# A planner's price table set anew: transposes, 1 MB loads, long ScalarE passes, strided copies, short products

## The chip, the cores and the metric

One core of a Trainium2 chip. The core has TensorE (PE in the profile, its weight loads PEld), VectorE (DVE), ScalarE (ACT), GpSimd (POOL) and SyncE (SP), which issues the DMAs. The metric is the device time of one launch in microseconds (us), as the median of several runs. The kernel computes in f32 accuracy with f16 products: a value is scaled by a power of two and held as a high and a low f16 half.

## The reference

Causal attention over 4 batches, 8 heads, 576 positions and 64 columns a head, with a bias, then two layers of a feed-forward kind on the 2304 resulting rows:

```
scores = q @ k.T / sqrt(64) + min(-(cum[i] - cum[j]), 0)       # cum = cumsum(max(s, 0)); causal
x = softmax(scores) @ v                                        # rows: 4 * 576 = 2304, columns: 8 * 64 = 512
h = x @ w_in ;  x2 = (h - tanh(h)) @ w_out                     # w_in 512 x 2048, w_out 2048 x 512
out = ((x2 @ w_a) * (x2 @ w_b)) @ w_out2                       # w_a, w_b 512 x 1536, w_out2 1536 x 512
```

The inputs are f32 or 64-bit arrays in DRAM; the weights arrive as 64-bit numbers, which the kernel turns into f32 itself.

## The kernel before

The work is a list of some thousands of operations, written out by `tile_attention_two_moes`: attention units (a batch and a pair of heads, in two parts: query blocks 0 and 1, and the later "merged" units with query blocks 2, 3 and the tail of 64), nine blocks of 256 rows through the first layer (`l1_mm`, `l1_act`, `l2_mm`), and five blocks of up to 512 rows through the second (`l3_mm`, `l3_act`, `l4_mm`, and `seven`, which computes products of a 2 x 2 split with seven instead of eight sub-products). Each weight is loaded in slots of 1 MB (`fetch`: the load, a pass that shifts the low halves, which may run on ScalarE or VectorE, a long pass on ScalarE, a joining pass on VectorE), squared on ScalarE for its scale, and split in two halves (`w_split`). `w2_done` closes the preparation of the second layer's weights; the products of the second layer wait for it. The second layer's weights live in a pool (`late`) that opens when the pool of the merged attention units (`rest`) has been used up.

In a unit, `u_split` makes the halves of q and k in the tile `qk`, a DMA transpose turns it into `qkT` (`u_turn`), a copy `kB` takes part of it, `u_qk` forms scores in PSUM, `u_exp` the exponentials (one block goes to the SBUF tile `zs`, the tail's lie in `z`), `u_norm` writes the two f16 halves to `a` (or `am` for the tail) by `copy_scaled` and `lo_part`, a second DMA transpose makes `aT` (`aTm`), and `u_pv` multiplies with `v` into 64 partitions of PSUM. `copy_scaled`, `lo_part` and `small` record calls that may run on one of two or three engines (`pl.either`).

No order is written out by hand. `Plan.record` stores each operation with what it depends on, a due time and its price from `cost` (line 575): how long it holds its engine, how long after that its result can be used (the lag), and for DMAs the time of the bytes. `Plan.run` (line 382) simulates the engines: of the operations that are ready on an engine, the one with the earliest due time that has its buffers goes next; for a call with several engines, `best` compares the time at which each would be through with it, by price times a weight (`WV`, `WV2` 1.2 for VectorE, `WP` 1.1 for GpSimd, 1 for ScalarE). For a DMA the lines are

```python
dma = max(dma, now + op.dur + 650.0) + op.size
end = dma
```

and what reads the result may start at `end + op.lag`. The order of this simulation is the order in which the instructions are issued on the chip, where each engine works through its own in that order and waits by semaphores.

Before the last simulation `Plan.refine` (line 322) goes through the list `REFINE`. For each step (gap, mix, shake, seed) it simulates the plan forwards, then backwards (`backward`, which finds the latest start of each operation, with `gap` added to the lags), and `move` shifts the due times by `mix` of the way to those latest starts and by a random amount of size `shake`; steps with a seed of 300 or more do so in a random stretch of time.

Of the kernel before, what the change touches and what calls it, by code (L numbers as in the profile page):

```python
# [12 lines left out]
F16 = mybir.dt.float16  # L13
# [21 lines left out]
MASKED = -1.0e34  # L35
BLOCKS = [(p, [b]) for p in range(2) for b in range(4)]
TURN = 0.0
REFINE = [(1000.0, 0.2, 0.0, 195), (1000.0, 0.1, 1000.0, 258), (200.0, 0.1, 1000.0, 286), (0.0, 0.1, 0.0, 402), (-200.0, 0.2, 1000.0, 73372), (100.0, 0.0, 2000.0, 21910), (100.0, 0.1, 3000.0, 984), (400.0, 0.5, 2000.0, 64535), (200.0, 0.1, 300.0, 792), (0.0, 0.0, 300.0, 70647), (2000.0, 1.0, 3000.0, 55229), (200.0, 0.0, 1000.0, 70112), (0.0, 0.05, 3000.0, 681), (-200.0, 0.0, 1000.0, 932), (2000.0, 0.1, 0.0, 724), (2000.0, 1.0, 0.0, 19448), (200.0, 0.0, 3000.0, 7485), (2000.0, 0.0, 2000.0, 26392), (400.0, 0.0, 1000.0, 851), (-200.0, 0.2, 300.0, 65873), (100.0, 0.0, 2000.0, 94663), (2000.0, 0.1, 300.0, 616), (400.0, 0.1, 0.0, 673), (2000.0, 0.2, 1000.0, 52138), (200.0, 0.5, 3000.0, 38807), (400.0, 0.0, 300.0, 20859), (100.0, 0.2, 0.0, 48173), (200.0, 0.3, 1000.0, 702), (200.0, 0.0, 300.0, 86139), (200.0, 0.05, 300.0, 39857)]
SEVEN = 12
GSB = (1,)  # L40
ZSB = 0
# [486 lines left out]
class _Eng:  # L528
# [3 lines left out]
    def __getattr__(self, what):  # L532
        plan, name = self.plan, self.name

        def call(*args, reads=(), writes=(), **kw):
            rd, wr = [], []
            for i, a in enumerate(args):
                if isinstance(a, View):
                    (wr if i == 0 else rd).append(a)
            for k, a in kw.items():  # L540
                if isinstance(a, View):
                    (wr if k in ("out", "accum_out") else rd).append(a)
            def real(a):
                assert not isinstance(a, View) or a.buf.real is not None, (name, what, a.buf.name, a.buf.tag)
                return a.real() if isinstance(a, View) else a

            def fn():
                return getattr(getattr(plan.nc, name), what)(  # L548
                    *[real(a) for a in args], **{k: real(a) for k, a in kw.items()})

            fn.what = (name, what)
            fn.lock = shares(name, what, rd, wr)
            dur, lag, size = map(round, cost(name, what, rd, wr, kw, args))
            plan.record(name, fn, rd, wr, reads, writes, dur, lag, size, plan.shift.get(name, 0.0))

        return call
# [18 lines left out]
def cost(eng, what, rd, wr, kw, args):  # L575


    def count(v):
        n = 1
        for d in v.shape[1:]:  # L580
            n *= d
        return n

    if not rd and not wr:
        return 500.0, 900.0, 1000.0
    main = wr[0] if wr else rd[0]
    n = max(count(v) for v in rd[:1] + wr[:1])
    if eng == "sync":
        rows = main.p1 - main.p0
        size = {F32: 4, I32: 4}.get(main.dtype, 2)  # L590
        b = rows * count(main) * size
        if what == "dma_start_transpose":
            return 650.0, 910.0, b / 292.5
        hold = 475.0 if rows in (32, 128) else 625.0
        return hold, 910.0, b / (180.0 if main.shape[-1] * size < 512 else 360.0)
    if eng == "tensor":
        lhs = rd[0]
        rate = 4.0 if lhs.dtype == F32 else 1.0
        cols = count(main)
        half = 0.62 if main.p1 - main.p0 == 64 else 1.0  # L600
        return max(cols * rate / 2.4 * half, 25.0) + 2, 200.0, 0
    psum = any(v.buf.pool == "ps" for v in rd)
    small = sum(isinstance(kw.get(k), View) for k in ("scale", "bias", "scalar", "scalar1", "scalar2"))
    if what == "tensor_scalar_mul" and isinstance(args[2], View):
        small += 1
    if eng == "vector":
        if what == "reciprocal":
            return 65 + 8 * n, 127.0, 0
        if what == "tensor_tensor_scan":
            return 65 + n, 127.0, 0  # L610
        fast = what.startswith("tensor_scalar") or what in ("tensor_single_scalar", "tensor_copy", "memset")
        rate = 0.96
        if fast and not psum:
            rate = 3.84 if rd and rd[0].dtype == F16 else 1.92
        return 69 + n / rate + 60 * small + 8 * ("accum_out" in kw), 127.0, 0
    if eng == "scalar":
        d = (52 if psum and not small else 94) + n / 1.2 + 93 * ("accum_out" in kw)
        return d + small * (51 if psum else 93), 153.0, 0
    if what == "tensor_tensor":
        return 149 + 1.9 * n, 80.0, 0  # L620
    if what == "tensor_scalar":
        return 190 + 83 * small + 0.833 * n, 80.0, 0
    if what == "memset":
        return 210.0, 80.0, 0
    return 70 + 1.45 * n, 80.0, 0
# [3 lines left out]
def tile_attention_two_moes(  # L629
# [1051 lines left out]
    with tc.manual_schedule():  # L1681
        pl.refine(REFINE)
        pl.run(switch)
# [34 lines left out]
```

## Time and profile before

| what | value |
|---|---|
| median of 3 runs | 1008.97 us (1007.15 to 1009.83) |
| the profiled execution's own time | 1005.35 us |
| its span, first to last instruction | 1003.5 us |
| TensorE busy | 916.8 us (91%) |
| VectorE busy | 815.2 us (81%) |
| ScalarE busy | 551.0 us (55%) |
| GpSimd busy | 148.6 us (15%) |
| granted TensorE clock, mean | 0.991 |
| DMA | 113.95 MB, mean 114 GB/s |

The span in 40 equal slices of 25 us; each digit is a busy share in tenths:

```
PE   1697889998989878989999989999999999999998
DVE  8698999979899989899999999999267559546545
ACT  6699668658768678778598764433022212222221
POOL 2033031102123212321001010020011002000000
```

TensorE is nearly full from 600 us on, where VectorE has room after 700 us; from 50 to 600 us both are close to full.

### The profile page before, as it was taken

To read this page: it belongs to the slowest core of one execution; us is meant where nothing else is said; L and a number is where in the kernel's file an instruction comes from. 1 tells how busy PE (TensorE), PEld (TensorE's weight loads), DVE (VectorE), ACT (ScalarE), POOL (GpSimd) and SP (SyncE) were. 2 spreads that over 40 slices of the span, in tenths; PEclk is the share of its full clock that TensorE was granted. 3 is DMA by queue.
4 is the path that set the end of the run, shared out by engine and by line. 5 is a ranking of instruction groups with operands and counts; after the bars stand their busy time and mean duration, and the time that the engine had idled before them with its cause. 6 is when DMAs were issued, how large, how long until landed. Compare 5 with 4: busy or idle time off the path is not lost.

```text
span 1003.5 us, 20812 instructions
## 1 busy us (share of the span) xinstructions
PE 916.8 (91%) x7998; PEld 689.4 (69%) x7998; DVE 815.2 (81%) x2058; ACT 551.0 (55%) x1097; POOL 148.6 (15%) x239
## 2 busy tenths in 40 slices
PE   1697889998989878999989999999999999999998
PEld 0485678887767756778778887644467777777675
DVE  8698999979899989999899999999267559546545
ACT  6699668658768678777598764433022212222221
POOL 2033031102123212321001010020011002000000
PEclk9997899999999999999999999999999999999999
DMA  8999767557986997996755530200011011000001
GB/s 227 221 329 225 184 109 140 104 113 152 177 161 129 194 183 158 181 181 135 233 171 198 180 106 2 63 22 1 1 42 43 1 43 42 1 2 12 32 1 43
DMA packets 282084, 113.95 MB, mean 114 GB/s; under 512 B 251200, under 2 KB 265776, under 8 KB 281984
## 3 DMA queue, kind: packets, MB, share of 16 engines
q1 hardware_dynamic: 281984, 112.62, 48.6%
q8 instruction: 62, 1.02, 0.4%
q14 instruction: 38, 0.31, 0.1%
HBM read 60.53 MB, written 11.17 MB: 71 GB/s over the span
## 4 chain that ended last, share of the span: by engine, by line
PE 39%; DVE 11%; ACT 4%; DMA 4%; issue 3%; SPq 0%; POOL 0%; DVEq 0%; POOLq 0%; ACTq 0%
PE h L548 14%; PE qk L548 12%; PE acc L548 8%; PE pv L548 6%; DVE w L548 2%; DVE xf L548 2%; ACT w L548 2%; DVE ghl L548 1%; DVE a L548 1%; DMA w<-in_moe_w_a_dram 1%; DVE qk L548 1%; DVE h L548 1%; DMA w<-in_moe_w_out_dram 1%; ACT xf L548 1%; DVE am L548 1%
## 5 line engine op out<-in xcount | busy, mean ns | idle before, releaser
L548 PEld LDWEIGHTS <-w 128*128 128x128 f16 x5160 | 498.5, 98 | 133.3 <-issue 30.2
L548 PE MATMUL h<-xhl,w 128*128 128x256 f16 (+1 forms) x2256 | 289.7, 279 | 3.9 <-DVE xhl L548 1.7
L548 PE MATMUL acc<-ghl,w 128*128 128x256 f16 x1536 | 187.6, 272 | 5.5 <-DVE ghl L548 2.2
L548 PE MATMUL h<-xf,w 128*128 128x256 f16 (+1 forms) x560 | 87.8, 306 | 0.7 <-ACT bits L548 0.4
L548 PEld LDWEIGHTS <-ghl 128*128 128x128 f16 x432 | 42.3, 98 | 44.6
L548 PEld LDWEIGHTS <-qkT 128*128 128x128 f16 (+2 forms) x352 | 28.5, 102 | 58.6 <-issue 33.5
L548 DVE CUSTOM_DVE_ANT_0 qk<-qk,caus,cs 128x384 f32<-128x384 f32 (+2 forms) x120 | 64.6, 555 | 2.2 <-PE qk L548 1.9
L548 PE MATMUL qk<-qkT 128*128 128x128 f16 (+4 forms) x168 | 45.7, 316 | 21.2 <-DMA qkT<-qk 7.6
L548 ACT ACTIVATE sq<-h 128x512 f32<-128x512 f32 x36 | 21.5, 597 | 78.2 <-PE h L548 78.2
L548 PE MATMUL acc<-w,ghl 128*128 128x512 f16 x252 | 60.9, 379 | 0.0
L548 ACT ACTIVATE qk<-qk,nm 128x512 f32<-128x512 f32 (+3 forms) x88 | 45.8, 521 | 18.7 <-DVE nm L548 15.1
L548 ACT ACTIVATE w<-w 128x1024 f32<-128x1024 f32 (+1 forms) x43 | 49.2, 1161 | 8.0 <-DMA w<-in_moe_w_out_dram 3.1
L548 ACT ACTIVATE th<-h,xc 128x512 f32<-128x512 f32 x64 | 43.9, 686 | 15.3 <-PE h L548 9.8
L548 DVE SCALAR_TENSOR_TENSOR a<-qk,sm,a 128x512 f16<-128x512 f32 (+3 forms) x88 | 48.8, 574 | 3.2 <-ACT a L548 2.9
L548 PE MATMUL qk<-kB,qkT 67*128 67x128 f16 (+4 forms) x168 | 45.5, 313 | 4.2 <-ACT kB L548 2.0
L548 ACT ACTIVATE sq<-raw 128x576 bf16<-128x576 f32 (+2 forms) x57 | 38.6, 679 | 18.1 <-DMA raw<-in_v_dram 7.5
L548 PEld LDWEIGHTS <-v 128*64 128x64 f16 x1440 | 38.4, 113 | 14.6 <-issue 13.2
L548 DVE TENSOR_TENSOR g<-g,h 128x512 f32<-128x512 f32 x36 | 24.4, 684 | 23.7 <-PE h L548 23.4
L548 PE MATMUL qk<-w,ghl 128*128 128x512 f16 x180 | 43.6, 379 | 0.0
L548 PE MATMUL pv<-aT,v 128*64 128x128 f16 x960 | 36.0, 225 | 5.3 <-DMA aT<-a 4.2
L548 ACT ACTIVATE bits<-h,cpc 128x512 f32<-128x512 f32 x18 | 12.4, 687 | 50.6 <-DVE g L548 37.7
L548 PEld LDWEIGHTS <-sq 128*128 128x128 f16 (+1 forms) x234 | 22.8, 98 | 23.9 <-ACT sq L548 0.8
(260 smaller groups left out, 1691.4 us busy)
## 6 DMA issues: line engine op xcount, KB each, us to landing
w<-in_moe_w_out_dram SPq DMA_DIRECT2D x8, 1024.0 KB
w<-in_moe_w_in_dram SPq DMA_DIRECT2D x6, 1024.0 KB
x_d<-x2hl SPq DMA_DIRECT2D x18, 256.0 KB
raw<-in_k_dram SPq DMA_DIRECT2D x32, 128.0 KB
raw<-in_v_dram SPq DMA_DIRECT2D x32, 128.0 KB
w<-in_moe_w_a_dram SPq DMA_DIRECT2D x4, 1024.0 KB
xhl<-x_d SPq DMA_DIRECT2D x4, 1024.0 KB
out_dram<-x2f SPq DMA_DIRECT2D x16, 256.0 KB
```

The lines of the kernel that those rows point to most:

```text
L548: return getattr(getattr(plan.nc, name), what)(*[real(a) for a in args], **{k: real(a) for k, a in kw.items()})
```

## The change

The price of a DMA transpose gets a lag of 1600 ns instead of 910, and that of a plain DMA of a million bytes or more 2000 instead of 910. A product whose result lies in 64 partitions has a least price of 12 ns instead of 25. On VectorE a single-source operation from f32 in SBUF to f16 whose last dimension is at most 128 counts one element a cycle instead of two. On ScalarE an operation of 1024 elements or more whose source is not in PSUM counts 95 ns more. The list of refinement steps is another one: 45 steps instead of 30. Operations, tiles, buffers and first due times are as before.

```diff
-REFINE = [(1000.0, 0.2, 0.0, 195), (1000.0, 0.1, 1000.0, 258), (200.0, 0.1, 1000.0, 286),
...
+REFINE = [(200.0, 0.2, 300.0, 133), (0.0, 0.1, 1000.0, 299), (0.0, 0.1, 300.0, 72),
...
         if what == "dma_start_transpose":
-            return 650.0, 910.0, b / 292.5
+            return 650.0, 1600.0, b / 292.5
         hold = 475.0 if rows in (32, 128) else 625.0
-        return hold, 910.0, b / (180.0 if main.shape[-1] * size < 512 else 360.0)
+        return hold, 910.0 if b < 1e6 else 2000.0, b / (180.0 if main.shape[-1] * size < 512 else 360.0)
...
         half = 0.62 if main.p1 - main.p0 == 64 else 1.0
-        return max(cols * rate / 2.4 * half, 25.0) + 2, 200.0, 0
+        return max(cols * rate / 2.4 * half, 25.0 if half == 1.0 else 12.0) + 2, 200.0, 0
...
         if fast and not psum:
             rate = 3.84 if rd and rd[0].dtype == F16 else 1.92
+            if rd and rd[0].dtype != F16 and main.dtype == F16 and main.shape[-1] <= 128:
+                rate = 0.96
         return 69 + n / rate + 60 * small + 8 * ("accum_out" in kw), 127.0, 0
     if eng == "scalar":
         d = (52 if psum and not small else 94) + n / 1.2 + 93 * ("accum_out" in kw)
+        d += 95 * (n >= 1024 and not psum)
         return d + small * (51 if psum else 93), 153.0, 0
```

## Rows read from the trace of the kernel before

**Rows 1.** Busy time by stretch: start:end, length, each engine's busy us (instructions), clock, DMA.

```profile
0.00:598.40 598.40, 516.90 (x5257) 421.39 (x5258) 544.29 (x1593) 444.60 (x905) 119.77 (x212) 0.99 0.78 176
598.40:1003.50 405.10, 399.93 (x2744) 268.01 (x2741) 270.93 (x466) 106.41 (x192) 28.85 (x27) 1.00 0.07 22
...
100.00:600.00 500.00, 454.40 (x4923) 374.86 (x4922) 460.74 (x1312) 363.93 (x736) 94.86 (x164) 0.99 0.74 160
...
490.00:600.00 110.00, 102.83 (x947) 89.90 (x946) 103.88 (x238) 85.22 (x115) 13.64 (x13) 1.00 0.56 189
```

**Rows 2.** Chain that ended last, 480 to 612 us: start, length, what.

```profile
489.15 9.51 DMA w<-in_moe_w_a_dram
...
534.70 7.13 DMA w<-in_moe_w_out_dram
...
553.22 5.73 DMA xf<-in_moe_w_out_dram
...
563.32 6.49 DMA xf<-in_moe_w_a_dram
...
595.99 0.32 DVE w2t L548
```

**Rows 3.** Instructions that use tile w: count, ns min/median/max, first and last start.

```profile
L548 PE MATMUL acc<-ghl,w x1536: 269/272/284, 133.2 to 598.3; 128*128 128x256 f16 x192
...
L548 PE MATMUL qk<-xhl,w x144: 272/326/379, 598.4 to 726.7; 128*128 128x256 f16 x72, 128*128 128x512 f16 x72
```

**Rows 4.** Who waited for whom, TensorE, 100 to 600 us: total us, times, longest.

```profile
PE qk L548 <- ACT zs L548: 5.0, 7, 1.5
PE pv L548 <- ACT xtail L548: 4.3, 4, 2.9
PE pv L548 <- DMA aT<-a: 4.2, 8, 1.1
...
PE qk L548 <- ACT kB L548: 1.5, 3, 0.9
...
PE qk L548 <- DMA qkT<-qk: 1.0, 2, 0.7
...
PE qk L548 <- DVE kB L548: 0.6, 1, 0.6
```

**Rows 5.** The same view, VectorE, 50 to 600 us.

```profile
DVE kB L548 <- DMA qkT<-qk: 5.4, 6, 1.6
...
DVE w L548 <- DMA w<-in_moe_w_b_dram: 2.1, 1, 2.1
```

**Rows 6.** Instructions in order, 405 to 425 us: start, length [idle before, releaser].

```profile
410.91 2.93 SPq L548 DMA_TRANSPOSE qkT<-qk  x1
...
413.02 0.66 PE L548 MATMUL pv<-aTm,v 128*64 128x64 f16 x30
...
417.58 0.45 DVE L548 TENSOR_SCALAR kB<-qkT 64x1152 f16<-64x1152 f16 x1 [0.81 <-DMA qkT<-qk]
```

**Rows 7.** Groups by form, ScalarE: count, busy us, mean ns, idle before.

```profile
L548 ACT ACTIVATE w<-w 128x1024 f32<-128x1024 f32 x31 | 35.9, 1162 | 3.1 <-DVE w L548 1.9 <-DMA w<-in_moe_w_b_dram 1.1
...
L548 ACT ACTIVATE w<-w 128x1024 int32<-128x1024 uint16 x12 | 13.9, 1160 | 4.9 <-DMA w<-in_moe_w_out_dram 3.1 <-DMA w<-in_moe_w_a_dram 1.5 <-DMA w<-in_moe_w_in_dram 0.3
```

**Rows 8.** Groups by form, VectorE.

```profile
L548 DVE TENSOR_SCALAR w<-w 128x1024 int32<-128x1024 int32 x9 | 6.2, 692 | 2.2 <-DMA w<-in_moe_w_b_dram 2.1
...
L548 DVE TENSOR_SCALAR a<-zs,sm 128x384 f16<-128x384 f32 x9 | 5.5, 608 | 0.1
L548 DVE TENSOR_SCALAR am<-z,sm 128x640 f16<-128x640 f32 x6 | 5.2, 871 | 0.0
...
L548 DVE TENSOR_SCALAR qk<-raw,sc 128x640 f16<-128x640 f32 x3 | 2.6, 873 | 0.0
...
L548 DVE TENSOR_SCALAR qk<-raw,sc 128x512 f16<-128x512 f32 x3 | 1.4, 478 | 0.0
```

**Rows 9.** Groups by form, GpSimd.

```profile
L548 POOL TENSOR_SCALAR am<-z,sm 128x640 f16<-128x640 f32 x4 | 3.2, 799 | 28.1 <-DVE sm L548 20.9 <-ACT x2f L548 7.2
```

More of the change, by code (lines that the diff above doesn't have):

```diff
@@ L37 @@
 TURN = 0.0
-REFINE = [(1000.0, 0.2, 0.0, 195), (1000.0, 0.1, 1000.0, 258), (200.0, 0.1, 1000.0, 286), (0.0, 0.1, 0.0, 402), (-200.0, 0.2, 1000.0, 73372), (100.0, 0.0, 2000.0, 21910), (100.0, 0.1, 3000.0, 984), (400.0, 0.5, 2000.0, 64535), (200.0, 0.1, 300.0, 792), (0.0, 0.0, 300.0, 70647), (2000.0, 1.0, 3000.0, 55229), (200.0, 0.0, 1000.0, 70112), (0.0, 0.05, 3000.0, 681), (-200.0, 0.0, 1000.0, 932), (2000.0, 0.1, 0.0, 724), (2000.0, 1.0, 0.0, 19448), (200.0, 0.0, 3000.0, 7485), (2000.0, 0.0, 2000.0, 26392), (400.0, 0.0, 1000.0, 851), (-200.0, 0.2, 300.0, 65873), (100.0, 0.0, 2000.0, 94663), (2000.0, 0.1, 300.0, 616), (400.0, 0.1, 0.0, 673), (2000.0, 0.2, 1000.0, 52138), (200.0, 0.5, 3000.0, 38807), (400.0, 0.0, 300.0, 20859), (100.0, 0.2, 0.0, 48173), (200.0, 0.3, 1000.0, 702), (200.0, 0.0, 300.0, 86139), (200.0, 0.05, 300.0, 39857)]
+REFINE = [(200.0, 0.2, 300.0, 133), (0.0, 0.1, 1000.0, 299), (0.0, 0.1, 300.0, 72), (400.0, 0.0, 300.0, 75513), (-200.0, 0.05, 1000.0, 951), (-200.0, 0.0, 3000.0, 352), (0.0, 0.0, 1000.0, 52630), (100.0, 0.1, 3000.0, 3375), (400.0, 0.0, 300.0, 2101), (-200.0, 0.05, 300.0, 720), (200.0, 0.2, 300.0, 947), (100.0, 0.0, 2000.0, 85557), (100.0, 0.0, 3000.0, 499), (2000.0, 0.05, 300.0, 82550), (0.0, 0.05, 2000.0, 59397), (200.0, 0.05, 300.0, 858), (200.0, 0.05, 300.0, 9783), (2000.0, 0.1, 1000.0, 12917), (2000.0, 0.0, 3000.0, 43288), (-200.0, 0.7, 300.0, 97992), (2000.0, 0.1, 1000.0, 88576), (0.0, 0.05, 2000.0, 16680), (400.0, 0.05, 0.0, 681), (2000.0, 0.0, 3000.0, 13189), (400.0, 0.5, 1000.0, 83050), (0.0, 0.1, 0.0, 867), (2000.0, 0.2, 0.0, 79911), (0.0, 0.3, 3000.0, 49215), (400.0, 0.2, 300.0, 875), (-200.0, 0.1, 3000.0, 74372), (200.0, 0.05, 0.0, 17593), (-200.0, 0.0, 2000.0, 9709), (0.0, 0.1, 300.0, 541), (0.0, 0.0, 1000.0, 662), (200.0, 0.0, 3000.0, 15867), (400.0, 0.05, 0.0, 701), (0.0, 0.05, 0.0, 50248), (2000.0, 0.2, 1000.0, 78338), (100.0, 0.3, 2000.0, 18751), (400.0, 0.0, 300.0, 15163), (100.0, 0.5, 300.0, 580), (100.0, 0.05, 0.0, 1286), (400.0, 0.0, 2000.0, 487), (0.0, 1.0, 2000.0, 79070), (100.0, 0.0, 3000.0, 3196)]
 SEVEN = 12
```

## The prediction

> **What bounds the kernel now.** I read the busy times by stretch first, then the chain of waits, then who waited for whom, then the single groups whose price the table changes.
>
> The busy times fall into two parts that meet at 598.4 us [rows 1]. After it TensorE is busy 399.9 of 405.1 us, and the other engines have room: nothing in that part gets shorter by another order, and whatever moves its beginning moves the end by as much. Before it TensorE is busy 516.9 of 598.4 us, idle 81.5, and VectorE 544.3, idle 54.1. Two engines are nearly full there, so an order that removes only TensorE's waits doesn't help where VectorE is late, nor the other way round.
>
> The chain of waits says what sets 598.4 us. From 489 to 596 us it runs through the preparation of the second layer's weights: 1 MB loads of 9.51, 7.13, 5.73 and 6.49 us between passes of ScalarE and VectorE, to `w2t`, the first step of `w2_done`, at 595.99 [rows 2]. The first layer's last `acc` product starts at 598.3 and the second's first `qk<-xhl` product at 598.4 [rows 3]. So the weights are ready some 2 us before TensorE runs out of first-layer work: both sides meet, and a gain needs both sooner.
>
> TensorE is idle 45.6 us of the 500 from 100 to 600 us [rows 1]. What ended its waits there is spread: ScalarE's `zs` 5.0 us, the transposes that make `aT` 4.2 and `qkT` 1.0, the copies `kB` behind the transposes 1.5 and 0.6; the largest of the other releasers, `xtail`, has 4.3 [rows 4]. VectorE lost 5.4 us on `qkT` and 2.1 on one 1 MB load [rows 5].
>
> **The change part by part.** No operation is added or taken away. Prices change, so the planner orders the same work otherwise and gives the calls that may run on two or three engines to others; 45 refinement steps instead of 30 then move the due times. I work against the profiled execution's own 1005.35 us (span 1003.5 and 1.85 around it).
>
> Transposes. The table counts 650 ns on the queue, 650 more, the bytes, and then the lag. A `qkT` of the later kind has 19 blocks of 32,768 bytes, 622,592 / 292.5 = 2128 ns; it was usable after 650 + 650 + 2128 + 910 = 4338 ns and is now after 5028. In the trace one issued at 410.91 let VectorE's `kB` start at 417.58, 6.67 us later, and left VectorE idle 0.81 [rows 6]. The new price is nearer, still short. What it can win on TensorE is the 4.2 + 1.0 + 1.5 + 0.6 = 7.3 us that hang on transposes [rows 4], where first-layer products stand ready to go ahead. On VectorE it is the 5.4 [rows 5]. Bounds: 7.3 down to nothing, if the products put ahead make the consumers of `qk` late instead. I take 4: 690 ns against a shortfall near 1 us on each, of the 7.3, cut once more since VectorE must follow.
>
> 1 MB loads. Usable after 475 + 650 + 2913 + 910 = 4948 ns before, 6038 now; the four on the chain took 5.73 to 9.51 [rows 2]. The first can't go earlier, because its pool opens when attention's closes. Of the others the planner can now order ScalarE's and VectorE's work so that nobody stands at a load; VectorE stood 2.1 us at one [rows 5]. Between -2 and +1 (loads then count as late and push others); I take -1.
>
> Long ScalarE passes. 1024 elements from SBUF were 94 + 853 = 947 ns, are 1042, and take 1162 and 1160; these two rows alone are 43 passes [rows 7]. ScalarE has slack over the first part, 444.6 of 598.4 us busy [rows 1], which hides the correction. I take 0. The bounds are -2 (consumers waiting less on ScalarE) and +7 (third rival).
>
> Strided copies. On VectorE a copy from f32 in SBUF to f16 whose last dimension is 128 or less is now priced at one element a cycle. `a<-zs` of 384: 329 before, 529 now, 608 in the trace, 9 calls; `am` of 640: 462, 796, 871, 6 calls; `qk` of 640: the same prices, 873, 3 calls [rows 8]. The plan missed 9 x 0.279 + 6 x 0.409 + 3 x 0.411 = 6.2 us of VectorE; now it misses 1.4. And with the weights 1.2 and 1.1 an `am` costs 955 on VectorE against 887 on GpSimd, where four such took 799 ns [rows 9], so copies leave VectorE when GpSimd or ScalarE is free. If half of the 18 go, VectorE sheds 9 x 0.75 = 6.8 us, but each copy's second half (`lo_part`) waits for it. Bounds -6.8 and 0; I take -2, as TensorE is the other wall and its waits ended by VectorE are small pieces.
>
> Here the row for three copies of 512 to `qk` speaks against the entry: they took 478 ns with a last dimension of 64 [rows 8], and are now priced 662. The Trainium skill, page "VectorE: DVE Perf Modes", section "What auto-detection actually checks", says that the two-port mode wants the outermost dimensions of source and destination in SBUF both even or equal; not the last dimension but odd counts of blocks (3, 5) would then be slow. The trace agrees: 608 for 3 blocks, 871 for 5, 478 for 4. By that rule the three even copies leave VectorE for no reason, 3 x 0.18 = 0.6 us, and the sum would be -6.4 instead of -7.
>
> Short products. 64 columns into 64 partitions were priced 27 ns, are 18.5; 30 of them took 0.66 us, 22 each [rows 6]. The error is as large as before with the other sign, 30 x 4 = 0.1 us a unit: 0.
>
> Refinement. All else that the new order does, of TensorE's 45.6 - 7.3 = 38.3 us of waits that no corrected price names [rows 1, 4]. The seeds tell nothing of its sign. I take 0, with 12.8 us (a third of them) either way as the bound.
>
> Sum: -4 - 1 + 0 - 2 + 0 + 0 = -7, that is 998.4 us for an execution like the profiled one. The median of the runs shown is 1008.97, 3.62 above the profiled one, so the forecast for a median is 1002. What would be late next: in 100 to 490 us VectorE's chain of `qk`, `a` and `am`, after it the weights.
>
> **The rivals.**
>
> Larger gain. More truthful prices let the refinement act on real waits, and a third of the 38.3 us goes besides: 1005.35 - 7 - 12.8 + 3.62 = 989. For it: TensorE's waits are many and short, with first-layer products at hand. Against it: VectorE has to follow, and from 490 to 600 us it has 6.1 us idle [rows 1].
>
> No change. The 7.3 us are a sixth of the waits; the corrected ones go and others come in the new order: 1006 to 1012. For it: the longest releaser, `zs` [rows 4], has no new price, and weights and first-layer work meet within 2 us [rows 2, 3], so half a gain is no gain.
>
> Slower. The pass that shifts the low halves of a weight (uint16 to int32) may run on ScalarE or VectorE. ScalarE's price goes from 947 to 1042, VectorE's stays 602 x 1.2 = 722. Twelve ran on ScalarE [rows 7]. If ten of them go to VectorE at 692 ns [rows 8], it gets 6.9 us more, and from 490 to 600 us it is already busy 103.9 of 110 [rows 1]. `w2_done` then comes that much later: 1005.35 + 6.9 + 3.62 = 1016. It decides as soon as `w2t` comes after the first layer's last product, and it is 2.3 us from that now. Against it: the planner compares when each engine would be free, and counts VectorE's queue.
>
> **How the numbers follow.** Forecast 0.42 (own range 997 to 1007), larger gain 0.15, no change 0.20, slower 0.23. A measurement tells 0.3% from no change, here 3 us, so faster is under 1005.9 and slower over 1012.0. Faster: 0.40 of the forecast and 0.15 of the larger gain, 0.55. Same: 0.02 of the forecast, 0.17 of the second rival, 0.01 of the third, 0.20. Slower: 0.22 of the third and 0.03 of the second, 0.25. The range is 986 to 1015: it leaves out about half of the third rival and the tail of the first.
>
> **What would show it.** Right: the second layer's first product starts near 591 us, the part after it again takes 405 us, TensorE's waits ended by `aT`, `qkT` and `kB` fall from 7.3 to about 3 us, VectorE's on `qkT` from 5.4 to 2, and fewer `am` and `a<-zs` copies of 384 run on VectorE. Step by step wrong: waits on transposes as long as before; the loads' pieces on the chain longer than their 28.9 us together; more uint16 passes on VectorE and `w2t` after the last first-layer product. The whole is wrong if the waits on transposes shrink and the second layer starts no sooner, or if the part after the meeting point changes its length.

## The result, and the profile after

The median after is 995.96 us (994.08 to 997.74, 4 runs) against 1008.22 for before in the same measurement: a ratio of 0.9877 [0.9853, 0.9901], 12.3 us less. The prediction had the direction right and about 60% of the size (-7); the result lies in its range of 986 to 1015, and just below the range of its own forecast, 997 to 1007. The profiled execution took 994.08 us, its span is 992.3; that of before is 11.2 longer.

Busy time by stretch, in the columns of [rows 1], with the new meeting point at 588.7:

```profile
0.00:588.70 588.70, 517.49 (x5269) 421.15 (x5270) 536.81 (x1603) 438.83 (x902) 137.64 (x218) 0.99 0.80 179
588.70:992.30 403.60, 398.17 (x2732) 266.82 (x2729) 270.21 (x473) 103.04 (x187) 21.05 (x18) 1.00 0.07 22
100.00:600.00 500.00, 467.41 (x4991) 383.77 (x4990) 456.97 (x1315) 364.99 (x737) 119.44 (x183) 0.98 0.74 160
490.00:600.00 110.00, 109.78 (x1009) 97.07 (x1010) 109.61 (x240) 86.12 (x121) 8.26 (x8) 1.00 0.45 150
```

The meeting point moved from 598.4 [rows 1] to 588.7: 9.7 of the 11.2 us. The part behind it is 1.5 shorter, and this is no gain of its own: it has 12 products fewer (2732 for 2744), which now run before the meeting, and 12 products take 1.31 us in the chain below. From 100 to 600 us TensorE was idle 45.6 us [rows 1] and is idle 500 - 467.41 = 32.6: 13.0 less. In the first 100 us its idle time rose, from 35.9 (81.5 - 45.6) to 38.6 (71.2 - 32.6). From 490 to 600 us TensorE and VectorE now both have under 0.5 us to spare. So about half of the 13.0, 7.0 us, lies behind 490 us, where attention's transposes are over: the last product that uses one starts at 487.2 before and at 476.0 after.

The products on tile w (columns of [rows 3]), and the two ends that meet, in order of time:

```profile
L548 PE MATMUL acc<-ghl,w x1536: 269/273/421, 132.2 to 588.6; 128*128 128x256 f16 x192
...
L548 PE MATMUL qk<-xhl,w x144: 272/326/379, 588.7 to 717.5; 128*128 128x256 f16 x72, 128*128 128x512 f16 x72
```

```profile
584.03 0.77 DVE L548 TENSOR_SCALAR cpc<-w2t,w2r 128x6 f32<-128x6 f32 x1
...
588.69 1.47 PE L548 MATMUL qk<-xhl,w 128*128 128x256 f16 x12
```

`w2_done`, which closes the preparation of the second layer's weights, ends with `cpc`, at 584.8, some 4 us before TensorE runs out of first-layer work. Before, these two stood the other way round:

```profile
598.37 1.47 PE L548 MATMUL qk<-xhl,w 128*128 128x256 f16 x12
598.81 0.22 DVE L548 TENSOR_SCALAR cpc<-w2t,w2r 128x6 f32<-128x6 f32 x1
```

So on the chip a product of the second layer doesn't wait for `w2_done`; only in the plan it does. What reads `cpc` is ScalarE's `th`, first at 600.2 before and 591.2 after. The `w2t` of 595.99 [rows 2], which is taken for the first step there, is the second. What moved is in the chain of waits from 480 to 612 us. Before, it lay on VectorE beyond the meeting point, to 608.8, and held four loads [rows 2]; after, one load is left, and from 571 us on it holds nothing but products. So the meeting point is now TensorE's own. The end of the stretch on VectorE before, then the chain after:

```profile
608.38 0.42 DVE g L548
...
608.84 1.47 PE h L548 x12
```

```profile
531.24 7.01 DMA xf<-in_moe_w_out_dram
...
571.74 2.65 PE acc L548 x23
...
588.85 1.31 PE qk L548 x12
```

Who waited for whom from 100 to 600 us, TensorE, answering to [rows 4]; then VectorE from 50 us on, for [rows 5]; then ScalarE at the 1 MB loads:

```profile
PE qk L548 <- DVE a L548: 5.1, 4, 3.5
PE qk L548 <- DVE nm L548: 4.8, 6, 2.1
...
PE pv L548 <- DMA aT<-a: 2.6, 4, 1.2
PE qk L548 <- ACT zs L548: 2.5, 3, 1.7
...
PE qk L548 <- DMA kB<-part_d: 1.7, 1, 1.7
PE qk L548 <- DMA qkT<-qk: 1.0, 2, 0.6
```

```profile
DVE kB L548 <- DMA qkT<-qk: 5.3, 6, 1.6
...
DVE ws L548 <- DMA ws<-in_moe_w_out_dram: 0.2, 1, 0.2
```

```profile
ACT w L548 <- DMA w<-in_moe_w_a_dram: 0.6, 1, 0.6
...
ACT xf L548 <- DMA xf<-in_moe_w_out_dram: 0.2, 1, 0.2
```

TensorE's waits on `aT`, `qkT` and `kB` fell from 7.3 [rows 4] to 3.6 us; the `kB` of the row with 1.7 is loaded from DRAM and hangs on no transpose. `zs` fell from 5.0 to 2.5, `xtail` on ScalarE from 4.3 out of the list. VectorE waits for `qkT` as long as before [rows 5]. So the direct waits gave 3.7 of the 13.0 us; most of the gain came off waits for other things.

The groups, answering to [rows 7 to 9]:

```profile
L548 DVE TENSOR_SCALAR w<-w 128x1024 int32<-128x1024 int32 x12 | 8.3, 688 | 0.1
...
L548 DVE TENSOR_SCALAR a<-zs,sm 128x384 f16<-128x384 f32 x5 | 3.0, 606 | 0.0
```

```profile
L548 ACT ACTIVATE w<-w 128x1024 int32<-128x1024 uint16 x9 | 10.6, 1177 | 0.8 <-DMA w<-in_moe_w_a_dram 0.6
L548 ACT ACTIVATE am<-z,sm 128x640 f16<-128x640 f32 x10 | 8.3, 826 | 5.6 <-DMA aTm<-am 3.3 <-issue 1.0 <-ACT z L548 1.0
```

```profile
L548 POOL TENSOR_SCALAR am<-z,sm 128x640 f16<-128x640 f32 x6 | 4.8, 798 | 19.9 <-ACT a L548 10.7 <-DVE sm L548 6.4 <-DMA aTm<-am 2.8
```

The six `am` and the three `qk` copies of 640 left VectorE, as did four of nine `a` copies. Three low-half passes (uint16 on ScalarE) went the other way, from 12 to 9 on ScalarE and from 9 to 12 on VectorE, which waits for loads no longer.

### The profile page after: what moved, and what is told of

It is laid out like the page before. It is cut to its first block, busy times and chain, and to the rows that moved or that the text cites. A ratio compares the mean times of both kernels' runs of the same rounds, so it can differ in the third digit from the quotient of the medians.

```text
span 992.3 us, 20822 instructions
## 1 busy us (share of the span) xinstructions
PE 915.7 (92%) x7998; PEld 688.0 (69%) x7998; DVE 807.0 (81%) x2075; ACT 541.9 (55%) x1089; POOL 158.7 (16%) x236
## 4 chain that ended last, share of the span: by engine, by line
PE 42%; DVE 10%; DMA 2%; issue 1%; ACT 1%; SPq 0%; DVEq 0%
PE h L548 15%; PE qk L548 12%; PE acc L548 9%; PE pv L548 6%; DVE w L548 3%; DVE ghl L548 1%; DMA qkT<-qk 1%; DVE h L548 1%; DMA xf<-in_moe_w_out_dram 1%; DVE xf L548 1%; DVE x2hl L548 1%; DVE a L548 0%; DVE g L548 0%; SPq L548 0%; DVE sq L548 0%
## 5 line engine op out<-in xcount | busy, mean ns | idle before, releaser
L548 PE MATMUL h<-xhl,w 128*128 128x256 f16 (+1 forms) x2256 | 297.1, 281 | 2.2 <-DVE g L548 1.7
L548 PE MATMUL acc<-ghl,w 128*128 128x256 f16 x1536 | 193.8, 274 | 3.9 <-DVE ghl L548 2.7
L548 PE MATMUL h<-xf,w 128*128 128x256 f16 (+1 forms) x560 | 85.3, 301 | 5.5 <-DVE w L548 3.8
L548 ACT ACTIVATE qk<-qk,nm 128x512 f32<-128x512 f32 (+3 forms) x88 | 45.6, 518 | 8.8 <-DVE nm L548 4.3
L548 PEld LDWEIGHTS <-v 128*64 128x64 f16 x1440 | 38.3, 113 | 16.9 <-issue 12.6
L548 DVE TENSOR_TENSOR g<-sq 128x256 f32<-128x256 f32 x36 | 14.6, 422 | 42.4 <-ACT sq L548 42.4
L548 ACT ACTIVATE w<-w 128x1024 f32<-128x1024 f32 (+1 forms) x40 | 45.7, 1166 | 0.9 <-DMA w<-in_moe_w_a_dram 0.6
L548 DVE SCALAR_TENSOR_TENSOR h<-h,xc,th 128x512 f32<-128x512 f32 x48 | 36.1, 752 | 6.9 <-ACT th L548 6.7
```

Of the source, the lines that this page charges most:

```text
L548: return getattr(getattr(plan.nc, name), what)(*[real(a) for a in args], **{k: real(a) for k, a in kw.items()})
```

## The experiments

The planner's simulation ends with a time of its own, which the kernel's code computes. It is no time on the chip, but it is the number that a list of steps is chosen by. The table has it beside the chip's median, with the distance between the two.

| label | prices | steps | planner's end | median, us | distance | ratio to before, 95% |
|---|---|---|---|---|---|---|
| before | old | 30 | 962.3 | 1008.22 | 45.9 | |
| after | new | 45 | 960.1 | 995.96 | 35.9 | 0.9877 [0.9853, 0.9901] |
| old5 | old | before's first 5 | 987.8 | 1024.84 | 37.0 | 1.0164 [1.0135, 1.0194] |
| new5 | new | after's first 5 | 987.6 | 1023.92 | 36.3 | 1.0161 [1.0128, 1.0195] |
| old13 | old | before's first 13 | 974.8 | 1018.03 | 43.2 | 1.0085 [1.0057, 1.0114] |
| new19 | new | after's first 19 | 975.6 | 1005.97 | 30.4 | 0.9982 [0.9964, 0.9999] |
| search_old_a | old | 36, searched | 960.8 | 1007.80 | 47.0 | 0.9998 [0.9981, 1.0016] |
| search_old_b | old | 44, searched | 962.4 | 1007.85 | 45.5 | 0.9993 [0.9974, 1.0012] |
| search_new_a | new | 43, searched | 964.3 | 997.03 | 32.7 | 0.9890 [0.9866, 0.9914] |
| search_new_b | new | 28, searched | 963.5 | 1001.01 | 37.5 | 0.9935 [0.9913, 0.9957] |
| search_landings | old, both new lags | 30, searched | 966.7 | 1000.54 | 33.8 | 0.9933 [0.9906, 0.9960] |
| search_engines | old, new engine prices | 38, searched | 967.3 | 1011.20 | 43.9 | 1.0024 [1.0008, 1.0041] |
| search_loads | old, new 1 MB lag | 42, searched | 963.1 | 1007.49 | 44.4 | 0.9982 [0.9966, 0.9998] |
| longer_search | new | after's 45 and 20 more | 951.7 | 992.11 | 40.4 | 0.9832 [0.9812, 0.9851] |

The kernels were run in five measurements, in which the median of before lay between 1007.61 and 1009.33; each ratio is to the before of the same one.

**Prices or steps?** The obvious crossing, one table with the other's list, has no order: either way the steps lead the simulation to a state in which operations hold each other's buffers. So the lists were cut where both planners' own ends are alike, once after 5 steps and once after 13 and 19.

```diff
-REFINE = [(1000.0, 0.2, 0.0, 195), (1000.0, 0.1, 1000.0, 258), ...
+REFINE = ...    # old5, old13: its first 5 or 13 steps, in before
+REFINE = ...    # new5, new19: the first 5 or 19 of after's list, in after
```

> The kernel before with only its first 5 refinement steps (prices of before). The planner's own end, which is no chip time, is 987.8 us; with all 30 steps it is 962.3, with the prices and 45 steps of after 960.1. The medians lie 45.9 us above the planner's end before (1008.2) and 35.9 above it after (996.0). Theory P (truer prices make the chip hold what the plan promises): 987.8 + 45.9 = 1034 us, about 10 us slower than the five-step kernel with the new prices. Theory S (the gain is the longer search alone, the prices change nothing): the distance is some 41 us for both tables, 1029 us, within 3 us of the five-step kernel with the new prices.

> The kernel after with only its first 5 refinement steps (prices of after); the planner's own end is 987.6 us, the same as that of the kernel before with 5 steps. Theory P: 987.6 + 35.9 = 1024 us. Theory S: 1029 us. Either way it is slower than both full kernels, if the planner's end means anything on the chip.

> The kernel before with its first 13 steps; the planner's own end is 974.8 us. Theory P: 974.8 + 45.9 = 1021 us. Theory S: 974.8 + 41 = 1016 us, equal to the 19-step kernel with the new prices within 3 us.

> The kernel after with its first 19 steps; the planner's own end is 975.6 us, 0.8 above the 13-step kernel with the old prices. Theory P: 975.6 + 35.9 = 1012 us, 9 us faster than that one. Theory S: 1016 us.

After 5 steps the two tables make no difference (1024.84 and 1023.92, at planner's ends of 987.8 and 987.6). At ends of 974.8 and 975.6 they differ by 12.1 us. Neither theory had this: neither do the prices carry the gain by themselves, nor are the steps worth the same under either table. The distance points to a third: it is equal at the start, and as steps are added it grows under the old prices (37.0, 43.2, 45.9) and does not under the new (36.3, 30.4, 35.9). The reading of it, for one list under each table: a step stays in a list because the planner's end falls; under wrong prices part of what falls is error, and the chip doesn't give it back.

**Equal effort.** To take the given lists out of it, lists were searched anew in the same way for both tables: from an empty list, random steps of the same kinds, kept where the planner's end falls, for the same number of minutes (3100 to 3600 tries), with two random starts.

```diff
-REFINE = [(1000.0, 0.2, 0.0, 195), ...
+REFINE = [(0.0, 0.3, 0.0, 130), ...        # search_old_a, search_new_a: one start
+REFINE = [(-200.0, 0.1, 300.0, 157), ...   # search_old_b, search_new_b: the other
```

> Prices of before, refinement steps searched anew by one procedure (random steps, kept when the planner's own end falls, the same time for each of the four kernels): planner's end 960.8 us. So far the median lay above the planner's end by 37.0 (5 steps), 43.2 (13) and 46.1 us (all 30) with the old prices, by 36.3 (5), 30.4 (19) and 35.9 (all 45) with the new ones. Theory U (a search under wrong prices uses their errors, and the chip gives back only part): 960.8 + 45 = 1006 us. Theory S (the distance doesn't depend on the prices): 960.8 + 38 = 999. Theory L (the list of after is a lucky one, lists scatter more than prices matter): anywhere from 995 to 1010, in no order.

> Prices of after, steps searched anew by the same procedure with the same random start: planner's end 964.3 us. Theory U: 964.3 + 34 = 998 us, faster than both searches under the old prices although the planner's end is the latest of the four. Theory S: 1002. Theory L: 995 to 1010.

> As search_old_a with another random start: planner's end 962.4 us. Theory U: 1007 us. Theory S: 1000. Theory L: 995 to 1010.

> As search_new_a with another random start: planner's end 963.5 us. Theory U: 997 us. Theory S: 1001. Theory L: 995 to 1010.

Under the old prices both searches end where before is (1007.80 and 1007.85); under the new, 10.8 and 6.8 us lower, though the planner's ends are 1 to 3.5 us higher. That is theory U, whose four numbers are met within 2 us but for search_new_b, 4 us later. So before's list was no unlucky one, and after's is not the main reason of the gain. Nor is the clock: the mean granted clock of the executions is 0.988 and 0.986 in the searches under the old prices, 0.988 and 0.988 under the new. The stretch from 100 to 600 us in search_old_a (its profiled execution is the slowest of its ten), then in search_new_a:

```profile
100.00:600.00 500.00, 457.89 (x4867) 374.49 (x4865) 456.75 (x1301) 359.05 (x735) 102.66 (x179) 0.97 0.75 160
```

```profile
100.00:600.00 500.00, 462.82 (x4972) 383.09 (x4971) 459.61 (x1312) 359.65 (x733) 114.84 (x175) 0.98 0.73 160
```

TensorE has 42.1 us idle and 37.2. What it and the others stood at there, first in search_old_a, then in search_new_a:

```profile
PE qk L548 <- DMA qkT<-qk: 11.7, 7, 2.5
...
DVE kB L548 <- DMA qkT<-qk: 11.3, 8, 2.3
...
ACT qk L548 <- DMA qkT<-qk: 11.3, 5, 5.1
...
ACT w L548 <- DMA w<-in_moe_w_out_dram: 3.9, 2, 3.7
```

```profile
PE qk L548 <- DMA qkT<-qk: 0.6, 1, 0.6
...
DVE kB L548 <- DMA qkT<-qk: 3.9, 4, 1.7
...
ACT xf L548 <- DMA xf<-in_moe_w_b_dram: 1.9, 1, 1.9
```

**Which prices?** Three searches of the same kind, each with a part of the new table: both lags of the DMAs, the prices of TensorE, VectorE and ScalarE, and the lag of the 1 MB loads alone (4842 tries).

```diff
-            return 650.0, 910.0, b / 292.5
+            return 650.0, 1600.0, b / 292.5               # search_landings
-        return hold, 910.0, ...
+        return hold, 910.0 if b < 1e6 else 2000.0, ...    # search_landings, search_loads
+        return max(cols * rate / 2.4 * half, 25.0 if half == 1.0 else 12.0) + 2, 200.0, 0   # search_engines
+                rate = 0.96                               # search_engines
+        d += 95 * (n >= 1024 and not psum)                # search_engines
```

> Prices of before, but for the two new lags (transposes 1600 ns, 1 MB loads 2000 ns); steps searched anew by the same procedure and for the same time: planner's end 966.7 us. Under the old prices the median lay 46.1, 47.0 and 45.5 us above the planner's end, under all the new ones 35.9, 32.7 and 37.5. Theory D (the landings carry the difference, engines wait at them by semaphores): 966.7 + 36 = 1003 us. Theory E (the time that ScalarE and VectorE are held carries it): 966.7 + 45 = 1012. Theory H (half each): 1007.

> The counterpart: prices of before, but for the new ones of long ScalarE passes, strided copies and short products; steps searched in the same way: planner's end 967.3 us. Theory D: 967.3 + 45 = 1012 us. Theory E: 967.3 + 36 = 1003. Theory H: 1008.

> Prices of before, but for the one new lag of 1 MB loads (2000 ns); steps searched by the same procedure (4842 tries, where the others had 3100 to 3600): planner's end 963.1 us. Medians lay 45.5 to 47.0 us above the planner's end with the old prices, 43.9 with the new engine prices alone, 33.8 with both new lags, 32.7 to 37.5 with all new prices. Theory 1M (the loads are the greater part: in the four kernels that price them at 910 ns ScalarE and VectorE stood 6 to 16 us at such loads between 100 and 600 us, in the four at 2000 ns 1 to 3): 963.1 + 36 = 999 us. Theory T (the transposes are): 963.1 + 45 = 1008. Theory H (each about half): 1003.

The lags alone give 1000.54, within the two full searches; the engine prices alone 1011.20, no better than before and if anything worse (1.0024 [1.0008, 1.0041]); the loads' lag alone 1007.49, 1.8 us better than before in the ratio and within 0.4 of the searches under old prices. Even the 1.8 can be the clock's: its executions had a mean granted clock of 0.994, those of before beside them 0.988, and before's own took 1010.5 us on average where the clock was 0.983 to 0.985, 1007.3 where it was 0.990 to 0.993 (9 and 19 of its 69 executions; the clock as a share of full speed). So the landing times carry the gain, and the loads' part is small, each seen in one list. What is left, the transposes' lag, by itself or with the loads', follows from this by subtraction; it was not run alone. Of the theories named before the runs, D (1003 and 1012) and T (1008) come within 3 us.

TensorE's idle time says where. Its us in the profiled executions, before and behind 490 us:

| transposes' lag | kernel | 100 to 490 us | 490 to 600 us |
|---|---|---|---|
| 910 | before | 38.4 | 7.2 |
| 910 | search_old_a | 36.5 | 5.6 |
| 910 | search_old_b | 38.2 | 6.7 |
| 910 | search_engines | 36.0 | 7.3 |
| 910 | search_loads | 42.4 | 5.6 |
| 1600 | after | 32.4 | 0.2 |
| 1600 | search_new_a | 33.7 | 3.5 |
| 1600 | search_new_b | 33.4 | 5.6 |
| 1600 | search_landings | 31.5 | 8.9 |
| 1600 | longer_search | 31.2 | 1.4 |

Up to 490 us, where the transposes are, the two groups stand apart, by 2 to 11 us. Behind it they mix, and there the 7.0 us by which after gained can't be put down to the lag. The cut lists don't all keep to it: old13 has 32.3 us up to 490, under the old lag.

Summed over TensorE, VectorE and ScalarE from 100 to 600 us, the waits that a transpose ended are 43.6, 19.5, 23.0 and 22.6 us in the four searches with the old lag for them (old_a, old_b, engines, loads), and 8.3, 13.1 and 13.7 in the three with the new one (new_a, new_b, landings). Those that a 1 MB load ended are 8.7, 16.4 and 11.8 under the old lag (old_a, old_b, engines) and 1.6 to 3.0 under the new (loads, new_a, new_b, landings). Between these searches each lag takes away the waits that it prices. It is no rule: longer_search, the fastest of all, has 20.8 and 6.0 under the new lags. search_loads against search_landings shows which of them the end hangs on; ScalarE's waits, first in search_loads, then in search_landings:

```profile
ACT kB L548 <- DMA qkT<-qk: 12.9, 8, 3.1
...
ACT w L548 <- DMA w<-in_moe_w_b_dram: 0.5, 1, 0.5
```

```profile
ACT kB L548 <- DMA qkT<-qk: 4.8, 5, 1.9
...
ACT w L548 <- DMA w<-in_moe_w_a_dram: 1.2, 1, 1.2
```

**A longer search.** The run has 20 more steps behind after's 45, under the new prices.

```diff
-REFINE = [(200.0, 0.2, 300.0, 133), ...
+REFINE = ...    # the same 45, and 20 more that lower the planner's end
```

> The kernel after, its 45 steps kept, and 20 more found by searching on under the same prices: planner's end 951.7 us instead of 960.1. If the distance stays at the 35.9 us of after, 988 us, 8 faster than after. If a further search under prices that are still not true (transposes above all) is lost in the same way as under the old ones, the distance grows by as much as the end falls, and it stays at 996.

The planner's end fell by 8.4 us, the chip's median by 3.9, to 992.11: the fastest version. That is between the two numbers named before. Its distance is up again, 35.9 to 40.4, as it would be if under the new prices too a search begins to live on what is still wrong. From 100 to 600 us TensorE's busy time is the same as after, and its meeting point is at 588.2:

```profile
100.00:600.00 500.00, 467.41 (x5012) 385.07 (x5011) 451.33 (x1299) 369.58 (x759) 127.88 (x198) 0.99 0.76 161
```

## Why the prediction was right, and what it mis-sized

**The bound** was read rightly in the main: two parts, the meeting point moves the end one for one (9.7 of 11.2), the part behind keeps its length but for 12 products. What sets the meeting point was not: it took the weights to be ready 2 us before, from the second step of `w2t`, where `w2_done` ended 0.7 us behind it without holding TensorE there.

**Transposes, -4.** The waits that it named fell by 3.7, as sized. The reason for the size was off: the transpose of [rows 6] was usable 6.67 - 4.34 = 2.3 us later than its old price, not 1, and the new lag covers 0.7 of that. VectorE's 5.4, which were to fall to 2, stayed at 5.3; over all three engines the waits ended by transposes from 100 to 600 us rose in this pair, 16.1 to 21.6, most of it on ScalarE, which has slack. Between equal searches they fell. So the pair alone doesn't show by which waits this lag paid, and adding up the waits at the transposes is no measure of what its price is worth.

**1 MB loads, -1.** Of the four pieces on the chain one is left, the waits at loads fell from 6.3 to 1.0; search_loads puts the whole at 1.8 [0.2, 3.4], at a higher granted clock than before had.

**Long ScalarE passes, 0; short products, 0; strided copies, -2.** VectorE's busy time fell by 8.2 us, more than the -6.8 taken as the bound, but search_engines, with 810.1 us of VectorE to the 815.2 of before, shows no gain by the three prices together: the -2 is the step that failed there. That copies leave VectorE was right, and the worth was not, as far as one list can show.

The working of this step also misread a column. A row's mean holds a tail that the next instruction on the engine overlaps, while the table prices the time from one start to the next. VectorE in order, before:

```profile
414.43 0.87 DVE L548 TENSOR_SCALAR am<-z,sm 128x640 f16<-128x640 f32 x1
415.22 0.75 DVE L548 CUSTOM_DVE_ANT_0 qk<-qk,caus,cs 128x512 f32<-128x512 f32 x1
```

From start to start it is 790 ns for `am` where the new price says 796: it misses nothing, where the prediction had a rest of 75 a copy from the 871 of [rows 8]. The entry that it doubted is wrong indeed:

```profile
125.48 0.47 DVE L548 TENSOR_SCALAR qk<-raw,sc 128x512 f16<-128x512 f32 x1
125.88 0.14 DVE L548 TENSOR_SCALAR xt<-xt 128x1 int32<-128x1 int32 x1
```

That is 400 ns for a copy that the entry catches as well (its last dimension is 64), of an even count of blocks; the old price was 396, the new is 662. By the Trainium skill ("VectorE: DVE Perf Modes", "What auto-detection actually checks") an even count of blocks on both sides keeps the fast mode; the trace agrees, with 400 for 512 elements (even) and 790 for 640 (5 blocks of 128), but not each time: of the two even copies of 256 to `qk` in after one takes 0.27 us from start to start, the other, at 57.05 beside a copy on GpSimd, 0.40. What this entry costs in time no run shows.

**Refinement, 0.** This is the term that was mis-sized: "The seeds tell nothing of its sign. I take 0, with 12.8 us (a third of them) either way as the bound." The seeds don't, but the prices do, in part. The rest of TensorE's waits fell from 38.3 to 32.6 - 3.6 = 29.0, by 9.3, within that bound. Of that 7.0 lies behind 490 us and may be the list's own. The searches show that the seeds are not all: the four under the transposes' old lag end at 1007.5 to 1011.2 us, the three under the new one at 997.0 to 1001.0. What fits this, though no run isolates it: 30 to 44 steps chosen under a lag that the chip exceeds build an order that the chip can't keep, and the loss appears at whatever is next in line. A wrong price then costs more than the waits that it names. That the sum came as near as it did is partly luck: its -2 has no worth that a run shows, and most of the gain stood in a term of 0.

**The rivals.** The larger gain (989) had the mechanism, "more truthful prices let the refinement act on real waits", and too large a size; the result lies between it and the forecast. No change is out: the zs row without a price of its own halved. The third was there in small, three passes instead of ten, and did not decide: `w2_done` ended 4 us ahead of the meeting point, and its ending behind it, as before, had not held TensorE's first product either.

**The signs named.** The second layer began at 588.7 for "near 591"; the waits on `aT`, `qkT` and `kB` came to 3.6 for "about 3"; copies left VectorE. VectorE's waits on `qkT` were the one that failed.

**What stays open.** Each list is one sample: two searches under one table lie 0.05 us apart (old) and 4.0 (new). So of the 12.3 us some 7 to 11 belong to the prices by the equal searches, some 6 by TensorE's idle time up to 490 us in this pair (38.4 to 32.4), and the rest can be the list's. The transposes' lag without the loads', and the even copies at their old price, were not run.

## What to carry to other kernels

Where an order is searched by a planner's own estimate, compare that estimate with the chip for a short and a long list: if the distance grows as steps are added, suspect a price that is too low, and expect part of any further search to be lost until it is mended. Mend first the latencies that the critical engine's inputs hang on, here the landing of transposes: the corrected engine prices by themselves gained nothing. Judge a price by several lists searched alike, since one list scatters by 4 us. Read an instruction's hold from start to start of neighbours, not from its duration.

## What the runs showed of the hardware

These transposes land later than even the new price says, and by very different amounts. After, from its issue to its first use by an engine that stood waiting:

```profile
62.88 3.67 SPq L548 DMA_TRANSPOSE qkT<-qk  x1
...
71.46 0.61 POOL L548 TENSOR_SCALAR kB<-qkT 64x512 f16<-64x512 f16 x1 [0.45 <-DMA qkT<-qk]
```

```profile
431.28 3.17 SPq L548 DMA_TRANSPOSE qkT<-qk  x1
...
437.69 0.45 DVE L548 TENSOR_SCALAR kB<-qkT 64x1152 f16<-64x1152 f16 x1 [0.71 <-DMA qkT<-qk]
```

It is 8.58 us in the first, a transpose of the earlier kind with 12 blocks, where the new price says 650 + 650 + 1344 + 1600 = 4244 ns, and 6.41 in the second, of 19 blocks, where it says 5028. The smaller one took longer: a single lag doesn't fit both.

ScalarE passes of 1024 elements from SBUF don't all hold the engine for the same time. Before:

```profile
514.94 1.06 ACT L548 ACTIVATE sq<-x2f 128x1024 bf16<-128x1024 f32 x1
515.89 1.12 ACT L548 ACTIVATE xf<-xf 128x1024 f32<-128x1024 f32 x1
516.90 0.69 ACT L548 ACTIVATE th<-h,xc 128x512 f32<-128x512 f32 x1
```

It is 0.95 us from start to start for the first and 1.01 for the second: the old price, 947, fits the one, the new, 1042, is nearer the other. So the new entry fits the passes of `fetch` and prices the squares too high. The type of the output is not what sets them apart: with 640 elements a pass that writes f32 and one that writes f16, both with a scalar operand per partition, take 0.72 and 0.74 us from start to start.

```profile
315.84 0.81 ACT L548 ACTIVATE z<-z,nm 128x640 f32<-128x640 f32 x1
316.56 0.19 ACT L548 ACTIVATION_READ_ACCUMULATOR z<-z,nm 128x1 f32 x1
...
317.63 0.83 ACT L548 ACTIVATE am<-z,sm 128x640 f16<-128x640 f32 x1
318.37 0.67 ACT L548 ACTIVATE th<-h,xc 128x512 f32<-128x512 f32 x1
```

In the code the passes of `fetch` read and write every second 32-bit word and the squares read neighbours; whether this is the reason no run shows.
